# Windowed attention, forward and backward: y and z turned by a DMA transpose, the two products of dx stacked to K=128, eight PSUM banks in one ring

## The chip, the cores and the metric

The kernel runs on one core of one Trainium2 chip. The metric is the device time of one execution in microseconds (us), as a median over several executions. PSUM is the memory that PE writes its products to; the program hands it out as eight banks, and PE waits when no bank is free (before the change `pw` waited so 127 times, 40.0 us in all, for ACT to empty one). Engines: PE is TensorE, PEld its weight load, DVE is VectorE, ACT is ScalarE, POOL is GpSimd, SP is SyncE. SP computes nothing here; it issues DMA transfers. "SPq" in a profile line means that SP's sequencer is occupied.

## The reference, cut to what matters

The image is 256 x 256 tokens of 384 channels in bf16, cut into 1024 windows of 64 tokens.

```
qkv = xw @ wqkv                                    # xw: [1024 windows, 64, 384]
q, k, v = thirds of qkv
p = softmax(q k^T * 384**-0.5)
out = (p @ v) @ wo
# outputs: out, and the gradients for x, wqkv and wo, given grad_out
```

## The kernel before

Weights are merged at the start: A = wq wk^T * scale and B = wv wo. Write x for a window's tokens, g for its grad_out, P for the softmax and dS for the gradient of the scores. Then

- y is x A turned, z is g B^T turned, and u = x B, v = x A^T. y and z come out of PE as channels by tokens.
- scores are y^T x (for P) and z^T x (for dP).
- out = P u (PSUM tile `po`), and dx = P^T z + dS^T y + dS v, three products in one PSUM tile (`pd`). U = dS x (`pu`) and W = P^T g (`pw`) feed the weight gradients, which a "filler" stage accumulates (`pg`).

A tile is two windows (128 tokens) and a quad is four tiles. There are 128 quads, and each takes one step of a software pipeline. Scores need y and z as channels by tokens; `pd` needs them as tokens by channels. Before the change PE turned them, 24 transposes of 128x128 a quad, and DVE copied each group of three out of PSUM:

```python
def yz_tok(st, t, part):
    src, dst = ((st["yz"][:, :, t, 1:3, :], st["yq"]), (st["zc"][:, :, t, :, :], st["zq"]))[part]
    pt = ring.tile([P, CK, P], BF16, tag="r")
    for m in range(CK):
        nc.tensor.transpose(pt[:, m, :], src[:, m, :, :].rearrange("p w k -> p (w k)"), ident[:])
    nc.vector.tensor_copy(out=dst[:, t, :].rearrange("p (m c) -> p m c", m=CK), in_=pt[:])
```

Attention works on halves of 64 partitions. Four matmuls of the 64x64 array shape run side by side (their starts are within 0.01 us in the timeline below), two "straight" and two "crossed"; I call that a slot. A tile has three slots:

```python
both((po, "PT", "uq", True, True), (pd, "Pb", "zq", True, False))
... # po -> osb on ACT -> out_0, one DMA on SP
both((pu, "ST", "xq", True, True), (pd, "Sb", "yq", False, False))
... # pu -> Uq on DVE
both((pw, "Pb", "dq", True, True), (pd, "ST", "vq", False, True))
... # pd -> dsb on ACT -> out_1, two DMAs on POOL; pw -> Wq on DVE
```

The loads of a quad are four of x (SP) and four of grad_out (POOL), 96 KB each. Two DMA transposes on SP turn them into `xT` and `dT`.

Of the kernel before, what the change touches and what calls it, by code (L numbers as in the profile page):

```python
# [9 lines left out]
ALU = mybir.AluOpType  # L10
# [12 lines left out]
def kernel(  # L23
# [33 lines left out]
    qp = ctx.enter_context(tc.tile_pool(name="qp", bufs=2))  # L57
    sm = ctx.enter_context(tc.tile_pool(name="sm", bufs=2))
    ob = ctx.enter_context(tc.tile_pool(name="ob", bufs=3))
    ps_sd = ctx.enter_context(tc.tile_pool(name="ps_sd", bufs=1, space=bass.MemoryType.PSUM))  # L60
    ring = ctx.enter_context(tc.tile_pool(name="ring", bufs=7, space=bass.MemoryType.PSUM))

    ident = const.tile([P, P], BF16)
    make_identity(nc, ident[:])
# [43 lines left out]
        return ap[0, 2 * WIN * bp:2 * WIN * (bp + 1), WIN * t:WIN * (t + 1), :]  # L108

    LO, HI = slice(0, WT), slice(WT, P)  # L110

    def load(st):
        bp, t0 = st["at"]
        st["xq"] = xq = grp.tile([P, QUAD, C], BF16, tag="xq", name="xq", bufs=2 * GQ + 3)
        st["dq"] = dq = qp.tile([P, QUAD, C], BF16, tag="dq", name="dq", bufs=5)
        for t in range(QUAD):
            nc.sync.dma_start(out=xq[:, t, :], in_=dram_tile(x, bp, t0 + t))
            nc.gpsimd.dma_start(out=dq[:, t, :], in_=dram_tile(grad_out, bp, t0 + t))  # L118
        st["xT"] = xT = qp.tile([P, QUAD, CK, P], BF16, tag="xT", name="xT", bufs=3)
        st["dT"] = dT = qp.tile([P, QUAD, CK, P], BF16, tag="dT", name="dT")  # L120
        for src, dst in ((dq, dT), (xq, xT)):
            nc.sync.dma_start_transpose(out=dst[:].rearrange("p t m k -> p (t m) k"),
                                        in_=src[:].rearrange("p t c -> p (t c)"))

    ENG = {"D": nc.vector.tensor_copy, "A": nc.scalar.copy}

    def project(st, kind, mo):
        if kind == 0 and mo == 0:
            st["yz"] = qp.tile([P, CK, QUAD, 4, WT], BF16, tag="yz", name="yz")
            st["zc"] = qp.tile([P, CK, QUAD, 2, WT], BF16, tag="zc", name="zc")  # L130
        yz = st["yz"]
        wgt, src = ((BT_sb, st["dT"]), (A_sb, st["xT"]))[kind]
        pj = ring.tile([P, QUAD, 2, WT], F32, tag="r")
        for m in range(CK):
            nc.tensor.matmul(pj[:].rearrange("p t w k -> p (t w k)"), lhsT=wgt[:, m, mo * P:(mo + 1) * P],  # L135
                             rhs=src[:, :, m, :], start=(m == 0), stop=(m == CK - 1))
        if kind == 0:
            ENG[EV["z"][mo]](out=yz[:, mo, :, 0:4:3, :], in_=pj[:])  # L138
            nc.vector.tensor_copy(out=st["zc"][:, mo, :, :, :], in_=yz[:, mo, :, 0:4:3, :])
        else:  # L140
            ENG[EV["y"][mo]](out=yz[:, mo, :, 1:3, :], in_=pj[:])  # L141

    def scores(st):
        yz, xT = st["yz"], st["xT"]
        st["sd"] = sd = ps_sd.tile([P, QUAD, 2, WT], F32, tag="sd", name="sd")
        for t in range(QUAD):
            for w in range(2):
                for m in range(CK):
                    nc.tensor.matmul(sd[:, t, w, :],  # L149
                                     lhsT=yz[:, m, t, 2 * w:2 * w + 2, :].rearrange("p s k -> p (s k)"),  # L150
                                     rhs=xT[:, t, m, w * WT:(w + 1) * WT],
                                     start=(m == 0), stop=(m == CK - 1))
# [4 lines left out]
    def soft(st, step):  # L157
# [14 lines left out]
        elif step == 3:  # L172
# [4 lines left out]
            nc.vector.reciprocal(out=ri[:], in_=rs[:])  # L177
            st["Pb"] = Pb = qp.tile([P, QUAD, WT], BF16, tag="Pb", name="Pb")
            nc.vector.tensor_tensor(out=Pb[:], in0=ex[:], in1=over_k(ri[:]), op=ALU.mult)
        elif step == 4:  # L180
            st["pr"] = pr = sm.tile([P, QUAD, WT], F32, tag="pr", name="pr")
            for w, h in ((0, LO), (1, HI)):
                nc.vector.tensor_tensor(out=pr[h, :, :], in0=sd[h, :, w, :], in1=st["Pb"][h, :, :], op=ALU.mult)
            st["D"] = D = sm.tile([P, QUAD], F32, tag="D", name="D")
            nc.vector.tensor_reduce(out=D[:], in_=pr[:], axis=AX.X, op=ALU.add)
        else:
            pd = sm.tile([P, QUAD, WT], F32, tag="pd")
            nc.vector.tensor_tensor(out=pd[:], in0=st["Pb"][:], in1=over_k(st["D"][:]), op=ALU.mult)
            st["Sb"] = Sb = qp.tile([P, QUAD, WT], BF16, tag="Sb", name="Sb")
            nc.vector.tensor_tensor(out=Sb[:], in0=st["pr"][:], in1=pd[:], op=ALU.subtract)  # L190

    def uv(st, t, part):
        if t == 0 and part == 0:
            for n in ("uq", "vq", "yq", "zq"):
                st[n] = qp.tile([P, QUAD, C], BF16, tag=n, name=n)
        wgt, dst, cp = ((B_sb, st["uq"], ENG[EV["u"][t]]), (AT_sb, st["vq"], ENG[EV["v"][t]]))[part]
        pj = ring.tile([P, C], F32, tag="r")
# [2 lines left out]
                             start=(m == 0), stop=(m == CK - 1))  # L200
        cp(out=dst[:, t, :], in_=pj[:])  # L201

    def yz_tok(st, t, part):
        src, dst = ((st["yz"][:, :, t, 1:3, :], st["yq"]), (st["zc"][:, :, t, :, :], st["zq"]))[part]
        pt = ring.tile([P, CK, P], BF16, tag="r")
        for m in range(CK):
            nc.tensor.transpose(pt[:, m, :], src[:, m, :, :].rearrange("p w k -> p (w k)"), ident[:])  # L207
        nc.vector.tensor_copy(out=dst[:, t, :].rearrange("p (m c) -> p m c", m=CK), in_=pt[:])

    def turn(st, kind):  # L210
        src, n = ((st["Pb"], "PT"), (st["Sb"], "ST"))[kind]
        st[n] = dst = qp.tile([P, QUAD, WT], BF16, tag=n, name=n)
        pt = ring.tile([P, QUAD, WT], BF16, tag="r")
        for t in range(QUAD):
            for h in (LO, HI):
                nc.tensor.transpose(pt[h, t, :], src[h, t, :], ident[h, h])  # L216
        nc.vector.tensor_copy(out=dst[:], in_=pt[:])

    def attend(st, t):
        bp, t0 = st["at"]  # L220
        if t == 0:
            st["Uq"] = grp.tile([P, QUAD, C], BF16, tag="Uq", name="Uq")
            st["Wq"] = grp.tile([P, QUAD, C], BF16, tag="Wq", name="Wq")
        po = ring.tile([P, C], F32, tag="r", name="po")
        pd = ring.tile([P, C], F32, tag="r", name="pd")
        pu = ring.tile([P, C], F32, tag="r", name="pu")
        pw = ring.tile([P, C], F32, tag="r", name="pw")

        def both(straight, crossed):
            for h, o, (dst, lhs, rhs, first, last) in ((LO, LO, straight), (LO, HI, crossed), (HI, LO, crossed),  # L230
                                                       (HI, HI, straight)):
                nc.tensor.matmul(dst[o, :], lhsT=st[lhs][h, t, :], rhs=st[rhs][h, t, :], start=first, stop=last)  # L232

        both((po, "PT", "uq", True, True), (pd, "Pb", "zq", True, False))
        osb = ob.tile([P, C], BF16, tag="o")
        ENG[EV["o"][t]](out=osb[:], in_=po[:])  # L236
        nc.sync.dma_start(out=dram_tile(out_0, bp, t0 + t), in_=osb[:])
        both((pu, "ST", "xq", True, True), (pd, "Sb", "yq", False, False))
        ENG[EV["U"][t]](out=st["Uq"][:, t, :], in_=pu[:])  # L239
        both((pw, "Pb", "dq", True, True), (pd, "ST", "vq", False, True))  # L240
        dsb = ob.tile([P, C], BF16, tag="d")
        ENG[EV["d"][t]](out=dsb[:], in_=pd[:])  # L242
        for h, w in ((LO, 1), (HI, 0)):
            nc.gpsimd.dma_start(out=dram_tile(out_1, bp, t0 + t)[WIN * w:WIN * (w + 1)], in_=dsb[h, :])  # L244
        ENG[EV["W"][t]](out=st["Wq"][:, t, :], in_=pw[:])  # L245

    fill = []

# [19 lines left out]

    def step(c, b, a):

        def on(st):
            return (lambda f, *r: f(st, *r)) if st is not None else (lambda f, *r: None)
        C_, B, A = on(c), on(b), on(a)
# [5 lines left out]
        B(uv, 1, 0)  # L279
        B(uv, 1, 1)  # L280
        B(soft, 2)
        C_(attend, 0)
        B(soft, 3)
        C_(attend, 1)
        B(soft, 4)
        filler(1)
        B(uv, 2, 0)
        B(uv, 2, 1)
        B(soft, 5)
        B(uv, 3, 0)  # L290
        B(uv, 3, 1)
        for t in range(QUAD):
            B(yz_tok, t, 0)
            B(yz_tok, t, 1)
        C_(attend, 2)
        C_(attend, 3)
        B(turn, 0)
        B(turn, 1)
        for kind in range(2):
            for mo in range(CK):  # L300
                A(project, kind, mo)
        filler(1)

    EV = {"z": "AAA", "y": "DAD", "u": "AAAA", "v": "AAAA", "o": "AAAA", "U": "DDDD", "W": "DDDD", "d": "AAAA"}
    quads = [(bp, t0) for bp in range(NBP) for t0 in range(0, NT, QUAD)]
    sts = [{"at": q, "i": i} for i, q in enumerate(quads)]
    n = len(sts)
    AHEAD = 2
    with tc.manual_schedule(engines=MANUAL):
        for i in range(min(AHEAD, n)):  # L310
            load(sts[i])
        held = []
        get = lambda i: sts[i] if 0 <= i < n else None
        for i in range(-1, n + 1):
            if AHEAD <= i + AHEAD < n:
                load(sts[i + AHEAD])
            step(get(i - 1), get(i), get(i + 1))
            if i > 0:
                held.append(sts[i - 1])
# [65 lines left out]
```

## Time and profile before

| | before |
|---|---|
| median of 3 runs | 2295.58 us |
| period from scores to scores | 17.59 us, times 128 = 2251 us |
| PE stages of a period | u/v 3.99, filler 3.91, z and y 3.89, attention 3.13, y/z transposes 1.43, scores 0.70, P and dS transposes 0.53 |

The stage lengths are distances between the starts of stages in the PE timeline, averaged over the steady part. So each includes the wait, if any, before the next stage.

From the page: busy time of each engine, and the chain that ended last (the waits, followed back from the last instruction).

```profile
PE 2231.7 (97%) x22910; PEld 1334.9 (58%) x22910; DVE 1827.0 (80%) x4771; ACT 1259.5 (55%) x2701; POOL 867.2 (38%) x1542
...
PE 95%; ACT 3%; DVE 1%; issue 0%; DMA 0%; ACTq 0%
```

PE is the limit. The next view is PE's timeline in attention of tiles 0 and 1 (start, length, then the instructions).

```profile
1019.64 0.32 PE L232 MATMUL po<-uq,PT 64*64 64x384 bf16 x1
1019.64 0.33 PE L232 MATMUL pd<-zq,Pb 64*64 64x384 bf16 x2
1019.65 0.32 PE L232 MATMUL po<-uq,PT 64*64 64x384 bf16 x1
1019.80 0.32 PE L232 MATMUL pu<-xq,ST 64*64 64x384 bf16 x1
...
1020.45 0.32 PE L232 MATMUL pw<-dq,Pb 64*64 64x384 bf16 x1 [0.32 <-ACT osb L236]
```

From slot to slot it is 0.16 us (1019.64 to 1019.80), and the last slot comes 0.65 us after the one before it, because `pw` wants a PSUM bank that an ACT copy still has to empty. Instructions are listed as 0.32 us long, though the slots start 0.16 us apart, so the listed lengths overlap. Only the distances between starts count.

### The profile page before, as it was taken

What the parts mean: (1) busy time and instruction counts of PE and PEld (TensorE: products, weight loads), DVE (VectorE), ACT (ScalarE), POOL (GpSimd) and SP (SyncE); (2) the same over time, 40 slices, a digit from 0 to 9 for tenths busy, and PEclk for the clock granted to TensorE, in tenths of its full rate; (3) what the DMA queues carried; (4) which work ended last, traced back from release to release, by engine and by line L of the source; (5) the groups of instructions that cost most, each with busy time, mean ns of one, the idle gap of its engine ahead of it and who ended that gap; (6) DMA issues with size and microseconds to landing.
All of it is one profiled execution on the core that took longest, in us unless ns stands there. A gap on an engine that the chain in (4) does not pass through costs nothing.

```text
span 2293.8 us, 59316 instructions
## 1 busy us (share of the span) xinstructions
PE 2231.7 (97%) x22910; PEld 1334.9 (58%) x22910; DVE 1827.0 (80%) x4771; ACT 1259.5 (55%) x2701; POOL 867.2 (38%) x1542
## 2 busy tenths in 40 slices
PE   7999999999999999999999999999999999999998
PEld 4555555555555555555555555555555555555555
DVE  6878887888788878877887788778878887888786
ACT  4555555555555555555555555555555555555553
POOL 3443333334333343343334333433333343334332
PEclk9999999999999999999999999999999999999999
DMA  7666555665565556555656565656556655655542
GB/s 165 143 142 135 137 131 135 138 139 133 138 139 132 133 138 138 133 135 135 142 131 142 134 141 128 143 134 138 129 135 139 139 132 139 138 133 134 137 114 60
DMA packets 624475, 308.59 MB, mean 135 GB/s; under 512 B 458816, under 2 KB 607040, under 8 KB 624192
## 3 DMA queue, kind: packets, MB, share of 16 engines
q1 hardware_dynamic: 550064, 203.49, 42.1%
q0 software_dynamic: 73728, 101.02, 15.6%
q8 instruction: 179, 2.93, 0.5%
q14 instruction: 104, 0.85, 0.1%
q10 hardware_dynamic: 400, 0.29, 0.0%
HBM read 101.84 MB, written 101.84 MB: 89 GB/s over the span
## 4 chain that ended last, share of the span: by engine, by line
PE 95%; ACT 3%; DVE 1%; issue 0%; DMA 0%; ACTq 0%
PE pg L256 22%; PE pj L135 22%; PE pj L199 21%; PE pt L207 7%; PE po L232 5%; PE pw L232 5%; PE sd L149 4%; PE pd L232 3%; PE pu L232 2%; PE pt L216 2%; ACT osb L236 2%; PE pc L97 0%; ACT uq L201 0%; DMA w_sb<-in_wqkv_dram 0%; ACT vq L201 0%
## 5 line engine op out<-in xcount | busy, mean ns | idle before, releaser
L244 POOL DMA_DIRECT2D out_dram<-dsb x1024 | 575.9, 570 | 1388.2 <-ACT dsb L242 1365.6
L201 ACT CAST uq<-pj 128x384 bf16<-128x384 f32 x512 | 245.3, 479 | 635.1 <-PE pj L199 632.9
L256 PEld LDWEIGHTS <-xq 128*128 128x128 bf16 x3072 | 290.1, 98 | 217.3 <-issue 21.9
L199 PEld LDWEIGHTS <-xT 128*128 128x128 bf16 x3072 | 291.6, 98 | 182.3 <-issue 0.5
L239 DVE CAST Uq<-pu 128x384 bf16<-128x384 f32 x512 | 280.9, 549 | 80.2 <-PE pu L232 80.2
L236 ACT CAST osb<-po 128x384 bf16<-128x384 f32 x512 | 247.2, 483 | 163.0 <-PE po L232 146.2
L199 PE MATMUL pj<-B_sb,xT 128*128 128x384 bf16 x1536 | 333.5, 326 | 0.0
L199 PE MATMUL pj<-AT_sb,xT 128*128 128x384 bf16 x1536 | 333.3, 326 | 0.0
L118 POOL DMA_DIRECT2D dq<-in_grad_out_dram x512 | 291.8, 579 | 12.8 <-issue 11.4
L245 DVE CAST Wq<-pw 128x384 bf16<-128x384 f32 x512 | 279.4, 546 | 0.0
L138 ACT CAST yz<-pj 128x512 bf16<-128x512 f32 x384 | 225.1, 586 | 97.3 <-PE pj L135 81.6
L258 DVE TENSOR_TENSOR GF_acc<-pg,GF_acc 128x384 f32<-128x384 f32 x258 | 143.8, 557 | 167.7 <-PE pg L256 163.8
L256 PE MATMUL pg<-Uq,xq 128*128 128x384 bf16 x1536 | 271.2, 327 | 0.0
L135 PE MATMUL pj<-dT,BT_sb 128*128 128x512 bf16 x1152 | 270.8, 380 | 0.2
L256 PE MATMUL pg<-Wq,xq 128*128 128x384 bf16 x1536 | 270.5, 326 | 0.0
L135 PE MATMUL pj<-xT,A_sb 128*128 128x512 bf16 x1152 | 269.5, 379 | 0.0
L242 ACT CAST dsb<-pd 128x384 bf16<-128x384 f32 x512 | 251.9, 492 | 6.6 <-PE pw L232 0.3
L201 ACT CAST vq<-pj 128x384 bf16<-128x384 f32 x512 | 245.3, 479 | 4.3
L141 DVE CAST yz<-pj 128x512 bf16<-128x512 f32 x256 | 175.9, 687 | 55.4 <-PE pj L135 55.4
L232 PE MATMUL pw<-dq,Pb 64*64 64x384 bf16 x1024 | 179.7, 330 | 40.0 <-ACT osb L236 40.0
L232 PEld LDWEIGHTS <-ST 64*64 64x64 bf16 x2048 | 147.6, 104 | 113.0 <-issue 102.0
L232 PE MATMUL po<-uq,PT 64*64 64x384 bf16 x1024 | 203.5, 337 | 0.2
(72 smaller groups left out, 3487.6 us busy)
## 6 DMA issues: line engine op xcount, KB each, us to landing
xq<-in_x_dram SPq DMA_DIRECT2D x512, 96.0 KB, 3.1
dq<-in_grad_out_dram POOLq DMA_DIRECT2D x512, 96.0 KB, 2.8
out_dram<-osb SPq DMA_DIRECT2D x512, 96.0 KB, 2.7
out_dram<-dsb POOLq DMA_DIRECT2D x1024, 48.0 KB, 2.6
dT<-dq SPq DMA_TRANSPOSE x128, 4.0
xT<-xq SPq DMA_TRANSPOSE x128, 4.3
w_sb<-in_wqkv_dram SPq DMA_DIRECT2D x1, 864.0 KB, 5.7
out_dram<-dw_sb SPq DMA_DIRECT2D x1, 864.0 KB, 3.8
```

The source lines that it names most:

```text
L118: nc.gpsimd.dma_start(out=dq[:, t, :], in_=dram_tile(grad_out, bp, t0 + t))
L135: nc.tensor.matmul(pj[:].rearrange("p t w k -> p (t w k)"), lhsT=wgt[:, m, mo * P:(mo + 1) * P], rhs=src[:, :, m, :], start=(m == 0), stop ...
L138: ENG[EV["z"][mo]](out=yz[:, mo, :, 0:4:3, :], in_=pj[:])
L199: nc.tensor.matmul(pj[:], lhsT=st["xT"][:, t, m, :], rhs=wgt[:, m, :], start=(m == 0), stop=(m == CK - 1))
L201: cp(out=dst[:, t, :], in_=pj[:])
L232: nc.tensor.matmul(dst[o, :], lhsT=st[lhs][h, t, :], rhs=st[rhs][h, t, :], start=first, stop=last)
L236: ENG[EV["o"][t]](out=osb[:], in_=po[:])
L239: ENG[EV["U"][t]](out=st["Uq"][:, t, :], in_=pu[:])
L242: ENG[EV["d"][t]](out=dsb[:], in_=pd[:])
L244: nc.gpsimd.dma_start(out=dram_tile(out_1, bp, t0 + t)[WIN * w:WIN * (w + 1)], in_=dsb[h, :])
L245: ENG[EV["W"][t]](out=st["Wq"][:, t, :], in_=pw[:])
L256: nc.tensor.matmul(pw[:], lhsT=st["xq"][:, t, ma * P:(ma + 1) * P], rhs=st["UW"[f] + "q"][:, t, :], start=(i == 0), stop=(i == n - 1))
```

## The change

Intent: free PE of the 24 transposes and DVE of the copies. The DMA transpose works on the whole `yz` tile, whose token slots lie in the order z0 y0 y1 z1. Each turned block therefore holds z of a window in one half of the partitions and y in the other. P and dS are laid out the same way (`ps`), so that P^T z + dS^T y becomes one matmul with K=128. The changed core, with cuts marked:

```diff
-    ps_sd = ... bufs=1, PSUM          # a bank of its own for the scores
-    ring = ... bufs=7, PSUM
+    ring = ... bufs=8, PSUM
     # load
-            nc.gpsimd.dma_start(out=dq[:, t, :], in_=dram_tile(grad_out, bp, t0 + t))
+            nc.sync.dma_start(out=dq[:, t, :], in_=dram_tile(grad_out, bp, t0 + t))
     # project: no zc copies any more
+    def to_tokens(st):
+        st["tok"] = tok = qp.tile([P, CK, QUAD, 2, P], BF16, tag="tok", name="tok")
+        nc.sync.dma_start_transpose(out=tok[:].rearrange("p m t b k -> p (m t b) k"),
+                                    in_=st["yz"][:].rearrange("p m t s k -> p (m t s k)"))
     # soft, step 3
+            for w, h in ((0, LO), (1, HI)):
+                nc.scalar.copy(out=ps[h, w, :, :], in_=Pb[h, :, :])
     # soft, step 5
-            nc.vector.tensor_tensor(out=Sb[:], in0=st["pr"][:], in1=pd[:], op=ALU.subtract)
+            for w, h, o in ((0, LO, HI), (1, HI, LO)):
+                nc.vector.tensor_tensor(out=ps[o, w, :, :], in0=st["pr"][h, :, :], in1=pd[h, :, :], op=ALU.subtract)
     # attend, now for a pair of tiles
+        for t in pair:
+            pd = ring.tile([P, C], F32, tag="r", name="pd")
+            for w, o in ((0, HI), (1, LO)):
+                nc.tensor.matmul(pd[o, :], lhsT=st["ps"][:, w, t, :], rhs=st["tok"][:, :, t, w, :], start=True,
+                                 stop=False)
+        ... # then for each tile: (pu, po), (pw, pd += dS v) as two slots of 64x64
+                    nc.gpsimd.dma_start(...)     # out_0 and out_1, four stores of 48 KB a tile, all on POOL
     # step: u/v, z, filler, attention of tiles 2 and 3, P/dS transposes, y, transpose to tokens, filler,
     #       attention of tiles 0 and 1
-    EV = {..., "y": "DAD", ...}
+    EV = {..., "y": "AAA", ...}
-    AHEAD = 2
+    AHEAD = 3
```

The four loads of grad_out moved from POOL's queue to SP's, and the stores of out_0 from SP's to POOL's. Cut above: there is one more buffer for grad_out (6) and for x, and the transposes of x and grad_out are issued one step after their loads.

More of the change, by code (lines that the diff above doesn't have):

```diff
@@ L59 @@
     ob = ctx.enter_context(tc.tile_pool(name="ob", bufs=3))
-    ps_sd = ctx.enter_context(tc.tile_pool(name="ps_sd", bufs=1, space=bass.MemoryType.PSUM))
-    ring = ctx.enter_context(tc.tile_pool(name="ring", bufs=7, space=bass.MemoryType.PSUM))
+    ring = ctx.enter_context(tc.tile_pool(name="ring", bufs=8, space=bass.MemoryType.PSUM))
     ident = const.tile([P, P], BF16)
@@ L110, with load_turn @@
     LO, HI = slice(0, WT), slice(WT, P)
+    OTHER = {0: HI, WT: LO}
     def load(st):
         bp, t0 = st["at"]
-        st["xq"] = xq = grp.tile([P, QUAD, C], BF16, tag="xq", name="xq", bufs=2 * GQ + 3)
-        st["dq"] = dq = qp.tile([P, QUAD, C], BF16, tag="dq", name="dq", bufs=5)
+        st["xq"] = xq = grp.tile([P, QUAD, C], BF16, tag="xq", name="xq", bufs=2 * GQ + 4)
+        st["dq"] = dq = qp.tile([P, QUAD, C], BF16, tag="dq", name="dq", bufs=6)
         for t in range(QUAD):
             nc.sync.dma_start(out=xq[:, t, :], in_=dram_tile(x, bp, t0 + t))
-            nc.gpsimd.dma_start(out=dq[:, t, :], in_=dram_tile(grad_out, bp, t0 + t))
+            nc.sync.dma_start(out=dq[:, t, :], in_=dram_tile(grad_out, bp, t0 + t))
+    def load_turn(st):
+        xq, dq = st["xq"], st["dq"]
         st["xT"] = xT = qp.tile([P, QUAD, CK, P], BF16, tag="xT", name="xT", bufs=3)
@@ L121, in load, with grad_turn @@
         for src, dst in ((dq, dT), (xq, xT)):
-            nc.sync.dma_start_transpose(out=dst[:].rearrange("p t m k -> p (t m) k"),
-                                        in_=src[:].rearrange("p t c -> p (t c)"))
+            k = G_ON_PE if src is dq else 0
+            if k < QUAD:
+                nc.sync.dma_start_transpose(out=dst[:, k:].rearrange("p t m k -> p (t m) k"),
+                                            in_=src[:, k:].rearrange("p t c -> p (t c)"))
+    def grad_turn(st, t):
+        if t >= G_ON_PE:
+            return
+        pt = ring.tile([P, CK, P], BF16, tag="r")
+        for m in range(CK):
+            nc.tensor.transpose(pt[:, m, :], st["dq"][:, t, m * P:(m + 1) * P], ident[:])
+        nc.vector.tensor_copy(out=st["dT"][:, t, :, :], in_=pt[:])
     ENG = {"D": nc.vector.tensor_copy, "A": nc.scalar.copy}
@@ L129, in project @@
             st["yz"] = qp.tile([P, CK, QUAD, 4, WT], BF16, tag="yz", name="yz")
-            st["zc"] = qp.tile([P, CK, QUAD, 2, WT], BF16, tag="zc", name="zc")
         yz = st["yz"]
@@ L138, in project @@
             ENG[EV["z"][mo]](out=yz[:, mo, :, 0:4:3, :], in_=pj[:])
-            nc.vector.tensor_copy(out=st["zc"][:, mo, :, :, :], in_=yz[:, mo, :, 0:4:3, :])
         else:
             ENG[EV["y"][mo]](out=yz[:, mo, :, 1:3, :], in_=pj[:])
+    def to_tokens(st):
+        st["tok"] = tok = qp.tile([P, CK, QUAD, 2, P], BF16, tag="tok", name="tok")
+        nc.sync.dma_start_transpose(out=tok[:].rearrange("p m t b k -> p (m t b) k"),
+                                    in_=st["yz"][:].rearrange("p m t s k -> p (m t s k)"))
     def scores(st):
         yz, xT = st["yz"], st["xT"]
-        st["sd"] = sd = ps_sd.tile([P, QUAD, 2, WT], F32, tag="sd", name="sd")
+        st["sd"] = sd = ring.tile([P, QUAD, 2, WT], F32, tag="r", name="sd")
         for t in range(QUAD):
@@ L179, in soft @@
             nc.vector.tensor_tensor(out=Pb[:], in0=ex[:], in1=over_k(ri[:]), op=ALU.mult)
+            st["ps"] = ps = qp.tile([P, 2, QUAD, WT], BF16, tag="ps", name="ps")
+            for w, h in ((0, LO), (1, HI)):
+                nc.scalar.copy(out=ps[h, w, :, :], in_=Pb[h, :, :])
         elif step == 4:
@@ L188, in soft @@
             nc.vector.tensor_tensor(out=pd[:], in0=st["Pb"][:], in1=over_k(st["D"][:]), op=ALU.mult)
-            st["Sb"] = Sb = qp.tile([P, QUAD, WT], BF16, tag="Sb", name="Sb")
-            nc.vector.tensor_tensor(out=Sb[:], in0=st["pr"][:], in1=pd[:], op=ALU.subtract)
+            ps = st["ps"]
+            for w, h, o in ((0, LO, HI), (1, HI, LO)):
+                nc.vector.tensor_tensor(out=ps[o, w, :, :], in0=st["pr"][h, :, :], in1=pd[h, :, :], op=ALU.subtract)
     def uv(st, t, part):
         if t == 0 and part == 0:
-            for n in ("uq", "vq", "yq", "zq"):
+            for n in ("uq", "vq"):
                 st[n] = qp.tile([P, QUAD, C], BF16, tag=n, name=n)
@@ L201, in uv @@
         cp(out=dst[:, t, :], in_=pj[:])
-    def yz_tok(st, t, part):
-        src, dst = ((st["yz"][:, :, t, 1:3, :], st["yq"]), (st["zc"][:, :, t, :, :], st["zq"]))[part]
-        pt = ring.tile([P, CK, P], BF16, tag="r")
-        for m in range(CK):
-            nc.tensor.transpose(pt[:, m, :], src[:, m, :, :].rearrange("p w k -> p (w k)"), ident[:])
-        nc.vector.tensor_copy(out=dst[:, t, :].rearrange("p (m c) -> p m c", m=CK), in_=pt[:])
     def turn(st, kind):
-        src, n = ((st["Pb"], "PT"), (st["Sb"], "ST"))[kind]
+        n = ("PT", "ST")[kind]
         st[n] = dst = qp.tile([P, QUAD, WT], BF16, tag=n, name=n)
@@ L214, in turn, with attend @@
         for t in range(QUAD):
-            for h in (LO, HI):
-                nc.tensor.transpose(pt[h, t, :], src[h, t, :], ident[h, h])
+            for w, o, h in ((0, LO, HI), (1, HI, LO)):
+                if kind == 0:
+                    nc.tensor.transpose(pt[o, t, :], st["Pb"][o, t, :], ident[o, o])
+                else:
+                    nc.tensor.transpose(pt[o, t, :], st["ps"][h, w, t, :], ident[h, h])
         nc.vector.tensor_copy(out=dst[:], in_=pt[:])
-    def attend(st, t):
+    def attend(st, pair):
@@ L220, in attend @@
         bp, t0 = st["at"]
-        if t == 0:
+        if pair[0] == 0:
             st["Uq"] = grp.tile([P, QUAD, C], BF16, tag="Uq", name="Uq")
             st["Wq"] = grp.tile([P, QUAD, C], BF16, tag="Wq", name="Wq")
-        po = ring.tile([P, C], F32, tag="r", name="po")
-        pd = ring.tile([P, C], F32, tag="r", name="pd")
-        pu = ring.tile([P, C], F32, tag="r", name="pu")
-        pw = ring.tile([P, C], F32, tag="r", name="pw")
-        def both(straight, crossed):
-            for h, o, (dst, lhs, rhs, first, last) in ((LO, LO, straight), (LO, HI, crossed), (HI, LO, crossed),
-                                                       (HI, HI, straight)):
-                nc.tensor.matmul(dst[o, :], lhsT=st[lhs][h, t, :], rhs=st[rhs][h, t, :], start=first, stop=last)
@@ L234, in attend @@
-        both((po, "PT", "uq", True, True), (pd, "Pb", "zq", True, False))
-        osb = ob.tile([P, C], BF16, tag="o")
-        ENG[EV["o"][t]](out=osb[:], in_=po[:])
-        nc.sync.dma_start(out=dram_tile(out_0, bp, t0 + t), in_=osb[:])
-        both((pu, "ST", "xq", True, True), (pd, "Sb", "yq", False, False))
-        ENG[EV["U"][t]](out=st["Uq"][:, t, :], in_=pu[:])
-        both((pw, "Pb", "dq", True, True), (pd, "ST", "vq", False, True))
-        dsb = ob.tile([P, C], BF16, tag="d")
-        ENG[EV["d"][t]](out=dsb[:], in_=pd[:])
@@ L243, in attend @@
-        for h, w in ((LO, 1), (HI, 0)):
-            nc.gpsimd.dma_start(out=dram_tile(out_1, bp, t0 + t)[WIN * w:WIN * (w + 1)], in_=dsb[h, :])
-        ENG[EV["W"][t]](out=st["Wq"][:, t, :], in_=pw[:])
+        pds = []
+        for t in pair:
[3 more added lines that the diff above has]
+                                 stop=False)
+            pds.append(pd)
@@ new lines, in both @@
+        def both(t, straight, crossed):
+            for h, o, (dst, lhs, rhs, first) in ((LO, LO, straight), (LO, HI, crossed), (HI, LO, crossed),
+                                                 (HI, HI, straight)):
+                nc.tensor.matmul(dst[o, :], lhsT=st[lhs][h, t, :], rhs=st[rhs][h, t, :], start=first, stop=True)
+        for t, pd in zip(pair, pds):
+            po = ring.tile([P, C], F32, tag="r", name="po")
+            pu = ring.tile([P, C], F32, tag="r", name="pu")
+            pw = ring.tile([P, C], F32, tag="r", name="pw")
+            both(t, (pu, "ST", "xq", True), (po, "PT", "uq", True))
+            osb = ob.tile([P, C], BF16, tag="o")
+            ENG[EV["o"][t]](out=osb[:], in_=po[:])
+            ENG[EV["U"][t]](out=st["Uq"][:, t, :], in_=pu[:])
+            both(t, (pw, "Pb", "dq", True), (pd, "ST", "vq", False))
+            dsb = ob.tile([P, C], BF16, tag="d")
+            ENG[EV["d"][t]](out=dsb[:], in_=pd[:])
+            for dst, src in ((out_0, osb), (out_1, dsb)):
+                for h, w in ((LO, 1), (HI, 0)):
+                    nc.gpsimd.dma_start(out=dram_tile(dst, bp, t0 + t)[WIN * w:WIN * (w + 1)], in_=src[h, :])
+            ENG[EV["W"][t]](out=st["Wq"][:, t, :], in_=pw[:])
@@ L281, in step @@
         B(soft, 2)
-        C_(attend, 0)
         B(soft, 3)
-        C_(attend, 1)
-        B(soft, 4)
-        filler(1)
         B(uv, 2, 0)
         B(uv, 2, 1)
-        B(soft, 5)
+        for t in range(QUAD):
+            A(grad_turn, t)
         B(uv, 3, 0)
         B(uv, 3, 1)
-        for t in range(QUAD):
-            B(yz_tok, t, 0)
-            B(yz_tok, t, 1)
-        C_(attend, 2)
-        C_(attend, 3)
+        B(soft, 4)
+        for mo in range(CK):
+            A(project, 0, mo)
+        B(soft, 5)
+        filler(1)
+        C_(attend, (2, 3))
         B(turn, 0)
         B(turn, 1)
-        for kind in range(2):
-            for mo in range(CK):
-                A(project, kind, mo)
+        for mo in range(CK):
+            A(project, 1, mo)
+        A(to_tokens)
         filler(1)
-    EV = {"z": "AAA", "y": "DAD", "u": "AAAA", "v": "AAAA", "o": "AAAA", "U": "DDDD", "W": "DDDD", "d": "AAAA"}
+        B(attend, (0, 1))
+    G_ON_PE = 0
+    EV = {"z": "AAA", "y": "AAA", "u": "AAAA", "v": "AAAA", "o": "AAAA", "U": "DDDD", "W": "DDDD", "d": "AAAA"}
     quads = [(bp, t0) for bp in range(NBP) for t0 in range(0, NT, QUAD)]
@@ L311 @@
             load(sts[i])
+            if i < AHEAD - 1:
+                load_turn(sts[i])
         held = []
@@ L316 @@
                 load(sts[i + AHEAD])
+            if AHEAD - 1 <= i + AHEAD - 1 < n:
+                load_turn(sts[i + AHEAD - 1])
             step(get(i - 1), get(i), get(i + 1))
```

## The prediction

> **What bounds the kernel now.** TensorE. The page gives PE 97% busy, DVE 80%, ACT 55%, and the chain of waits is 95% PE. In the timeline the period from one scores stage to the next is 17.59 us (1016.38 to 1033.97); 128 quads make 2251 us, and about 42 us are prologue and tail. Per quad, by distances between starts in the PE timeline: scores 0.70 us, u/v 8 x 0.488 = 3.90, the gradient filler 2 x 1.95 = 3.90, projections 3.89, the y/z transposes 1.34 (24 x 56 ns), the P/dS transposes 0.53, and attention 12 slots of four 64x64 matmuls. A slot takes 0.16 us when nothing holds it (1.92 in all), but attention fills about 3.3 us: tiles 0 and 1 lose 0.48 us waiting for a PSUM bank (the pw matmul waits for the osb copy 127 times), and tiles 2 and 3 go at 0.26 us instead of 0.16, the pace of the DVE's eight yq/zq copies before them (started every 0.265 us), which free the banks.
>
> **What goes.** The y/z transposes, 1.34 us of PE; eight yq/zq copies (345 ns each) and three zc copies (294 ns); two 687 ns yz casts move to ACT. DVE falls from 14.2 to about 10 us a quad. The bank pacing, about 1.0 us of PE, should mostly go with it, helped by eight banks in one ring.
>
> **What stays.** Stacking saves no streaming time: the two pd products sat in slots that po and pu shared. Before, a tile needs three slots of four 64x64 matmuls; after, one of two 128x64 and two of four 64x64.
>
> **What comes.** (1) Two more changes of array shape per quad[...]. In this trace, entering or leaving attention shows 0.09 to 0.13 us extra, so I add 0.2 us. (2) ACT takes two 64x256 copies (estimate 0.4 us each) and two casts of 0.59 us: 9.9 to about 12 us. (3) One transpose of 768 KB per quad. The two existing ones (384 KB each) run at about 205 GB/s, 256-byte packets of 18 ns median, so some 3.9 us more DMA engine time: from roughly 9 to 13 us of a 16 us period. It is issued some 14 us before attention reads it, so its latency should not show. (4) out_0 moves to POOL: 16 issues of 0.57 us, 9.1 us. None becomes the longest engine.
>
> **Sum for PE.** Streaming 14.85 us, shape changes 0.5, left-over bank waits 0.3: 15.7 us. Times 128 plus 44: **2055 us**, 10% faster. Range 1985 to 2150. Chances: faster by over 2% 0.92, within 2% 0.05, slower 0.03.
>
> **What would show it right or wrong.** PE near 97% busy with a period near 15.7 us; no yq/zq/zc groups; DVE near 65%, ACT near 75%; attention slots at 0.16 us with the osb wait gone; the stacked pair of matmuls starting together; nobody waiting for the tok transpose; DMA share near 0.8.
>
> **What would make it wrong.** The two 128x64 matmuls of a tile not running side by side, or their weight loads not hidden: up to 0.16 us per tile, 80 us in all. DMA: if transposes, loads and stores slow each other, tok or xT/dT arrive late and PE waits, perhaps above 2150 us. ACT: the P copies sit in its queue before four u/v evictions and wait for DVE's softmax, which could run the banks out and stall PE.

The 0.2 us is my estimate from the 0.09 to 0.13 us that stand there (before the change, 1018.55 to 1019.13 us into attention, where three matmuls of u/v take 0.49 us; 1020.45 to 1020.74 out of it, where a slot takes 0.16). Point (2) does not say what its 0.4 us rests on. ACT's one operation of 256 elements took 0.42 us before the change (419 ns, L171), and the copies took 0.40 us in the changed kernel (403 ns, L198).

## More of the kernel before

The SP queue, from the view of one tile's instructions: shortest, median and longest issue in ns, then the start of the first and the last in us.

```profile
L122 SPq DMA_TRANSPOSE dT<-dq x128: 1435/1471/2642, 9.1 to 2213.8; - x128
L122 SPq DMA_TRANSPOSE xT<-xq x128: 1412/1665/3262, 11.0 to 2215.4; - x128
L117 SPq DMA_DIRECT2D xq<-in_x_dram x512: 552/598/2314, 1.3 to 2209.8; - x171
```

So each load holds SP for 0.60 us and a transpose of 12 blocks of 128x128 for 1.47 us (`dT`) or 1.67 us (`xT`), by the medians. Over a quad SP was issuing for 8.6 us out of 17.6 (the lengths of all its DMA instructions, added up).

## The result, and the profile after

The changed kernel takes 2143.5 us (median of 4 runs, 2137.1 to 2146.7) against 2295.9 us. The ratio is 0.9333, with a 95% interval of 0.9308 to 0.9358. Ratios here are the mean time of one kernel's fast runs over that of the other's of the same rounds, so not quite the ratio of the medians. The time lies inside the stated range, 88 us above the number that I gave.

Stage lengths a quad, computed from the traces as before, in us:

| | u/v | z | y | filler | attention | P/dS transp. | y/z transp. | scores | period |
|---|---|---|---|---|---|---|---|---|---|
| before | 3.99 | 1.95 | 1.94 | 3.91 | 3.13 | 0.53 | 1.43 | 0.70 | 17.59 |
| after | 4.42 | 1.97 | 1.94 | 4.09 | 2.84 | 0.38 | 0 | 0.70 | 16.33 |

Without any wait u/v takes 3.90 us, the least in this trace. So the changed kernel has a floor of about 15.8 us on PE, and 0.54 us is lost between u/v and z. The page after, in the same order as before:

```profile
PE 2029.8 (95%) x18814; PEld 1098.6 (51%) x18814; DVE 1379.5 (64%) x3235; ACT 1448.5 (68%) x3213; POOL 1137.8 (53%) x2054
...
DMA  8999999999999999999999999999999999999992
...
PE 41%; DMA 26%; SPq 15%; ACT 9%; issue 5%; POOL 1%; DVE 1%; ACTq 0%; POOLq 0%
DMA dT<-dq 20%; PE pj L147 16%; PE pj L219 10%; PE pg L278 9%; SPq L117 7%; SPq L118 7%; DMA out_dram<-osb 5%; ACT yz L150 4%; ACT osb L259 3%; PE sd L165 3%; POOL out_dram L266 1%; SPq L156 1%; DMA out_dram<-dsb 1%; ACT yz L152 1%; PE pd L244 1%
```

The chain that ended last is no longer PE's alone: it passes through the landing of `dT` and through SP's issue of loads (L117, L118). PE's timeline shows the place, the end of u/v and the start of z:

```profile
1023.46 0.65 PE L219 MATMUL pj<-AT_sb,xT 128*128 128x384 bf16 x3
1024.90 2.12 PE L147 MATMUL pj<-dT,BT_sb 128*128 128x512 bf16 x9 [0.79 <-DMA dT<-dq]
```

SP's timeline over one quad explains it:

```profile
1006.75 6.27 SPq L156 DMA_TRANSPOSE tok<-yz  x1
1013.06 0.59 SPq L117 DMA_DIRECT2D xq<-in_x_dram  x1
1013.69 0.60 SPq L118 DMA_DIRECT2D dq<-in_grad_out_dram  x1
1014.33 0.60 SPq L117 DMA_DIRECT2D xq<-in_x_dram  x1
1014.97 0.60 SPq L118 DMA_DIRECT2D dq<-in_grad_out_dram  x1
1015.61 0.60 SPq L117 DMA_DIRECT2D xq<-in_x_dram  x1
1016.26 0.60 SPq L118 DMA_DIRECT2D dq<-in_grad_out_dram  x1
1016.90 0.60 SPq L117 DMA_DIRECT2D xq<-in_x_dram  x1
1017.54 0.62 SPq L118 DMA_DIRECT2D dq<-in_grad_out_dram  x1
1018.20 2.17 SPq L127 DMA_TRANSPOSE dT<-dq  x1
1020.42 1.99 SPq L127 DMA_TRANSPOSE xT<-xq  x1
1022.51 5.35 SPq L156 DMA_TRANSPOSE tok<-yz  x1
```

There is no hole in it. Each issue starts 0.04 to 0.10 us after the one before it ends. From `tok` to `tok` it is 15.76 us here, and on average SP is inside a DMA instruction for 15.7 us of a period of 16.3; the gaps between eleven instructions make up the rest. The transposes that fill it take longer than they did before:

```profile
L127 SPq DMA_TRANSPOSE dT<-dq x128: 1439/2204/3315, 9.7 to 2076.3; - x128
L127 SPq DMA_TRANSPOSE xT<-xq x128: 1715/2778/4687, 11.4 to 2077.8; - x128
L156 SPq DMA_TRANSPOSE tok<-yz x128: 3603/5592/7426, 30.2 to 2099.0; - x128
```

Two more numbers that I computed from the trace say who waits for whom. The transpose to tokens starts on average 6.4 us after the last copy of y that it needs has ended, so SP is late and not y. And in 85 of 128 quads z starts within 0.1 us of the landing of `dT`.

A trap for readers of waits: the view of SP's waits puts 578 us of `tok` down to an ACT copy.

```profile
SPq L156 <- ACT yz L150: 578.1, 115, 6.3
```

That is a copy of z (L150) in the stage that runs meanwhile. The copies of y, on which the transpose depends, had long been done. The 5.0 us that it lists for each of the 115 is about as long as the issue of the transpose itself (5.5 us on average).

### The profile page after: what moved, and what is told of

It is laid out like the page before. It is cut to its first block, busy times and chain, and to the rows that moved or that the text cites. A ratio compares the mean times of both kernels' runs of the same rounds, so it can differ in the third digit from the quotient of the medians.

```text
span 2144.9 us, 50954 instructions
## 1 busy us (share of the span) xinstructions
PE 2029.8 (95%) x18814; PEld 1098.6 (51%) x18814; DVE 1379.5 (64%) x3235; ACT 1448.5 (68%) x3213; POOL 1137.8 (53%) x2054
## 3 DMA queue, kind: packets, MB, share of 16 engines
q8 instruction: 147, 2.41, 0.5%
## 4 chain that ended last, share of the span: by engine, by line
PE 41%; DMA 26%; SPq 15%; ACT 9%; issue 5%; POOL 1%; DVE 1%; ACTq 0%; POOLq 0%
DMA dT<-dq 20%; PE pj L147 16%; PE pj L219 10%; PE pg L278 9%; SPq L117 7%; SPq L118 7%; DMA out_dram<-osb 5%; ACT yz L150 4%; ACT osb L259 3%; PE sd L165 3%; POOL out_dram L266 1%; SPq L156 1%; DMA out_dram<-dsb 1%; ACT yz L152 1%; PE pd L244 1%
## 5 line engine op out<-in xcount | busy, mean ns | idle before, releaser
L266 POOL DMA_DIRECT2D out_dram<-osb x1024 | 571.9, 563 | 933.6 <-ACT osb L259 906.3
L278 PEld LDWEIGHTS <-xq 128*128 128x128 bf16 x3072 | 300.0, 98 | 226.8 <-issue 1.6
L147 PE MATMUL pj<-dT,BT_sb 128*128 128x512 bf16 x1152 | 276.6, 387 | 60.4 <-DMA dT<-dq 54.2
L221 ACT CAST vq<-pj 128x384 bf16<-128x384 f32 x512 | 250.2, 489 | 2.8 <-PE pj L219 0.5
L152 ACT CAST yz<-pj 128x512 bf16<-128x512 f32 x384 | 224.2, 585 | 32.0 <-PE pj L147 0.9
L150 ACT CAST yz<-pj 128x512 bf16<-128x512 f32 x384 | 208.4, 638 | 14.4 <-PE pj L147 13.3
L147 PEld LDWEIGHTS <-BT_sb 128*128 128x128 bf16 x1152 | 106.8, 99 | 207.2 <-DMA dT<-dq 92.2
L198 ACT COPY ps<-Pb 64x256 bf16<-64x256 bf16 x256 | 103.2, 403 | 149.6 <-DVE Pb L195 148.1
L251 PE MATMUL pu<-xq,ST 64*64 64x384 bf16 x1024 | 175.5, 336 | 0.0
```

The lines of the kernel that those rows point to most:

```text
L147: nc.tensor.matmul(pj[:].rearrange("p t w k -> p (t w k)"), lhsT=wgt[:, m, mo * P:(mo + 1) * P], rhs=src[:, :, m, :], start=(m == 0), stop ...
L150: ENG[EV["z"][mo]](out=yz[:, mo, :, 0:4:3, :], in_=pj[:])
L152: ENG[EV["y"][mo]](out=yz[:, mo, :, 1:3, :], in_=pj[:])
L221: cp(out=dst[:, t, :], in_=pj[:])
L251: nc.tensor.matmul(dst[o, :], lhsT=st[lhs][h, t, :], rhs=st[rhs][h, t, :], start=first, stop=True)
L266: nc.gpsimd.dma_start(out=dram_tile(dst, bp, t0 + t)[WIN * w:WIN * (w + 1)], in_=src[h, :])
```

## The experiments

Theories, stated before the first runs. Q: SP's queue, which issues one transfer after the other, has become a second bottleneck. D: the 16 DMA engines are full (the page's DMA row shows 9 everywhere). B: the lost time is a wait for PSUM banks or for ACT, since the trace also names ACT before z in places. All edits are to the changed kernel unless another is named.

### 1. The loads of grad_out back on POOL

```diff
-            nc.sync.dma_start(out=dq[:, t, :], in_=dram_tile(grad_out, bp, t0 + t))
+            nc.gpsimd.dma_start(out=dq[:, t, :], in_=dram_tile(grad_out, bp, t0 + t))
```

> The changed kernel with one line undone: the four dq loads of a quad are issued on POOL again, as before the change, so SP issues 4 loads and 3 transposes instead of 8 and 3. Theory Q (the SP queue, which issues one transfer after the other, is the co-bottleneck: 8 loads of 0.64 us and three transposes of together about 11 us make a loop of 16.1 us, longer than PE's own 15.8): the loop falls to 13.5 us, the dT wait of 0.54 us per quad goes, the period is PE's 15.8 us and the time 2075 us. Theory D (the 16 DMA engines themselves are full): same bytes and packets, so 2143 us within 1% and the dT wait stays. Theory B (the wait is for PSUM banks or ACT, as the chain also names ACT ps before the z projection): no change either.

Measured: 2082.5 us (2080.7 to 2085.8), ratio 0.9075, correct. SP is issuing for 12.2 us of a period of 15.9. Its timeline now has holes, 1003.10 to 1015.89 being the whole of its work for one quad:

```profile
1003.10 4.96 SPq L156 DMA_TRANSPOSE tok<-yz  x1
1008.10 2.53 SPq L117 DMA_DIRECT2D xq<-in_x_dram  x4
1010.80 2.13 SPq L127 DMA_TRANSPOSE dT<-dq  x1
1012.98 2.91 SPq L127 DMA_TRANSPOSE xT<-xq  x1
```

The transpose to tokens starts 0.03 us after the last y copy in every quad of the steady part, and `dT` lands in the median 9.1 us before z reads it, in no quad within 0.1 us. One line, with the same bytes moved, returns 61 of the 88 us. D, which expected no change, is refuted in the form that was stated, and the DMA row shows how little it tells. The windows view of 200 to 2000 us, for the changed kernel first and then for this run (last columns: granted clock, DMA share, GB/s):

```profile
200.00:2000.00 1800.00, 1725.93 (x16115) 933.52 (x16113) 1173.34 (x2754) 1238.80 (x2754) 978.08 (x1763) 1.00 1.02 195
```

```profile
200.00:2000.00 1800.00, 1761.07 (x16501) 962.61 (x16500) 1202.76 (x2825) 1263.16 (x2825) 1251.79 (x2260) 1.00 1.08 200
```

The share was above 1 in both (1.02 and 1.08), so the packet times that it adds up overlap, and it was higher in the faster run. Two things besides SP's time changed with that line: the loads went to POOL's own DMA queue, and there in fewer packets (the traces show 1536 and 4608 bytes where SP's loads have 768), so the expectation's "same bytes and packets" is half true. The engines' time did not fall with it, as the share shows. Run 4 keeps queue and packet size.

### 2. No transpose to tokens (wrong result)

```diff
-        st["tok"] = tok = qp.tile(...); nc.sync.dma_start_transpose(out=tok..., in_=yz...)
+        st["tok"] = tok_fixed            # set to zero once
```

> Wrong result on purpose: the changed kernel without the tok transpose; attention reads a tile of zeros that is set once. Everything else as it is. It takes the new DMA work away whole. Theories Q and D both expect the dT wait to go and about 2075 us (PE's own 15.8 us a quad). If the time stays near 2143 us (theory B), the missing half microsecond per quad has nothing to do with DMA.

Measured: 2070.2 us (2068.9 to 2071.6), ratio 0.902. As meant, out_1 (dx) is wrong and the other outputs are right. u/v to z is 3.92 us, and the period is 15.82. This is what PE can do in this arrangement; my number for it was 2055.

### 3. The same layout by PE transposes

```diff
-        nc.sync.dma_start_transpose(out=tok..., in_=yz...)
+        for t in range(QUAD):
+            for b in range(2):
+                pt = ring.tile([P, CK, P], BF16, tag="r")
+                for m in range(CK):
+                    nc.tensor.transpose(pt[:, m, :], yz[:, m, t, 2 * b:2 * b + 2, :]..., ident[:])
+                nc.vector.tensor_copy(out=tok[:, :, t, b, :], in_=pt[:])
     # called in one row after the z stage
```

> The changed kernel with the tok layout made by 24 PE transposes and 8 DVE copies per quad, as y and z were before, but in the stacked layout. It leaves the stacking, the order of the stages and the ring of eight banks, and takes the DMA transpose away. Expected by Q and D: PE 15.8 + 1.34 us of transposes, no dT wait, some bank waits behind the 8 copies of 0.35 us: period 17.1 to 17.5 us, 2250 to 2290 us, correct result. Then the new order and ring alone bring at most 2%, and the DMA transpose the rest. If it is below 2200 us, the order and ring bring more than I think.

Measured: 2331.8 us (2330.5 to 2335.4), ratio 1.0162, correct. That is above my range. The 24 transposes took 2.08 us where 24 x 56 ns make 1.34. Run 7 repairs this.

### 4. Four more issues on SP, no more bytes

```diff
-            nc.sync.dma_start(out=dq[:, t, :], in_=dram_tile(grad_out, bp, t0 + t))
+            for r in range(2):
+                nc.sync.dma_start(out=dq[WT * r:WT * (r + 1), t, :],
+                                  in_=dram_tile(grad_out, bp, t0 + t)[WIN * r:WIN * (r + 1)])
```

> The suspected cost doubled in part: the changed kernel with each of the four dq loads cut into two issues of 64 partitions on SP. Same bytes, same packet size, four more issues per quad. Theory Q: the SP loop grows by 4 x 0.64 us to about 18.7 us and the time to about 2440 us. Theory D: the engines have the same packets to move, so within 1% of 2143 us. Theory B: no change.

Measured: 2347.6 us (2343.6 to 2362.1), ratio 1.0239: slower than before the change, with the bytes of the changed kernel. An issue of half a load (0.63 us) costs as much as one of a whole load (0.60 us):

```profile
1009.21 1.26 SPq L119 DMA_DIRECT2D dq<-in_grad_out_dram  x2
```

The period is 17.96 us, where Q expected 18.7, so 1.6 of the 2.6 us came through. The rest was won back in the transposes: `tok` held SP for 4.9 us on average instead of 5.5. So the transposes' part of SP's loop is not a fixed cost. It gets shorter when they come further apart, which fits that SP waits in them for the DMA engines. No run shows that wait by itself. Two readings of the traces bear on it. In run 4, the quarter of the `tok` issues with the least other traffic in its first 3.6 us took 4.1 us on average and the quarter with the most 5.6; in the changed kernel these are 5.3 and 5.6. And in the changed kernel's `tok` shown above, the engines moved only 9 GB/s from 1011.0 to 1012.0 us, so full engines cannot be all of it.

### 5. Four staging buffers in place of three, with grad_out on POOL

```diff
 # on top of experiment 1
-    ob = ctx.enter_context(tc.tile_pool(name="ob", bufs=3))
+    ob = ctx.enter_context(tc.tile_pool(name="ob", bufs=4))
```

> The changed kernel with the dq loads on POOL (as in the first of the experiments) and four instead of three staging buffers for each output tile. In that first experiment 13 waits of PE, together about 15 us, were left, of 0.3 to 2.8 us each, and ACT waited 63 us for output stores to free a staging buffer. If those are the cause, the time falls from 2083 to about 2070 us, what the run without the tok transpose took. If not, it stays at 2083.

Measured: 2066.0 us (2063.0 to 2071.4), ratio 0.9003, correct. The period is 15.79 us. u/v to z is 3.90 us in every quad of the steady part, so no wait is left there.

### 6. Stacking undone, DMA transpose kept

With the slots in the order z0 y0 y1 z1, taking the stacked matmul apart would give a straight and a crossed product into one `pd` bank. The two straight products of `po` read different halves of the input partitions and write the two partition halves of one bank; their starts are 0.01 us apart (1019.64 and 1019.65 above), and the result is correct. No run here shows what the chip does when two such products write the same half. So DVE sorts the slots first, and all `pd` products are crossed, as before the change:

```diff
 # on top of experiment 5
+    def sort(st, kind):                       # zy holds z0 z1 y0 y1
+        for mo in range(CK):
+            nc.vector.tensor_copy(out=st["zy"][:, mo, :, 2 * kind:2 * kind + 2, :],
+                                  in_=st["yz"][:, mo, :, (slice(0, 4, 3), slice(1, 3))[kind], :])
-    in_=st["yz"]...                           # to_tokens
+    in_=st["zy"]...
-    two ACT copies into ps; two DVE subtracts into ps
     # yz has one buffer in place of two, to make room for zy
+    one DVE subtract into Sb
-    attend: pd, pd stacked; then (pu, po), (pw, pd) for each tile
+    attend: (pu, pd += P z) for both tiles; (po, pd += dS y) for both; (pw, pd += dS v) for both
```

> The kernel of the run above with the stacking undone and the DMA transpose kept: z and y are copied by the DVE (6 copies of about 0.29 us) into the order z0 z1 y0 y1, one DMA transpose turns them, and all three pd products are 64x64 matmuls beside po, pu and pw, as before the change. No array-shape change inside attention; pu is made and released first, so that the next stage finds a bank. Stage lengths in the changed kernel: attention takes 1.42 us a pair, of which 6 slots are 0.96; 0.13 goes for the change from 128x64 to 64x64 and about 0.16 for the bank wait at its end. If stacking only costs (my view), attention falls to about 1.15 us a pair and the time from about 2070 to about 2000 us. If stacking helps PE (the intent of the change), it rises above 2070 us.

Measured: 2033.0 us (2019.3 to 2049.7), ratio 0.8837, correct. The execution of 2049.7 us counts as slow, being 1.5% above the fastest; the ratio leaves it out, and the three others have a median of 2024.5 us. Attention falls from 2.84 to 2.41 us a quad, and the P/dS transposes rise from 0.38 to 0.48. The timeline of one pair after the change and the start of the next stage (instructions of one slot cut to the first):

```profile
1000.99 0.52 PE L244 MATMUL pd<-tok,ps 128*64 128x384 bf16 x4
1001.44 0.35 PE L251 MATMUL pu<-xq,ST 64*64 64x384 bf16 x1
...
1001.63 0.32 PE L251 MATMUL pw<-dq,Pb 64*64 64x384 bf16 x1
...
1001.79 0.32 PE L251 MATMUL pu<-xq,ST 64*64 64x384 bf16 x1
...
1001.95 0.32 PE L251 MATMUL pw<-dq,Pb 64*64 64x384 bf16 x1
...
1002.41 0.86 PE L165 MATMUL sd<-xT,yz 128*128 128x64 bf16 x24
```

And the same pair unstacked:

```profile
1003.60 0.35 PE L245 MATMUL pu<-xq,ST 64*64 64x384 bf16 x1
...
1003.79 0.32 PE L245 MATMUL pu<-xq,ST 64*64 64x384 bf16 x1
1003.95 0.32 PE L245 MATMUL po<-uq,PT 64*64 64x384 bf16 x1
...
1004.11 0.33 PE L245 MATMUL pd<-tok,Sb 64*64 64x384 bf16 x2
...
1004.27 0.32 PE L245 MATMUL pw<-dq,Pb 64*64 64x384 bf16 x1
...
1004.44 0.32 PE L245 MATMUL pw<-dq,Pb 64*64 64x384 bf16 x1
1004.78 0.86 PE L172 MATMUL sd<-xT,yz 128*128 128x64 bf16 x24
```

Stacked, the two 128x64 slots take 0.45 us before the first 64x64 slot starts, where the first two slots of the unstacked pair take 0.35 (1003.60 to 1003.95). I put the 0.10 down to the shape change. From the last slot to scores it is 0.46 us stacked and 0.34 unstacked. Both have six slots, and the pair takes 1.42 against 1.18 us. The unstacked run also releases its first bank earlier, and ACT has two copies less to make, so it shows shape change, order of the products, bank wait and ACT's relief together; no run separates them.

### 7. PE transposes, spread out

```diff
 # experiment 3, with its eight groups called one at a time:
+    after u/v tiles 1 and 2 (four groups), after each z projection (three), after soft 5 (one)
```

> The run with the PE transposes again (2332 us, above what I expected), with the eight groups of transposes spread between the u/v and z stages instead of in one row behind z. There the row of 24 took 2.05 us instead of the 1.34 that 24 x 56 ns make, and that 0.7 us a quad is the excess. If it is only the wait for banks behind the evictions, the period falls from 17.9 to about 17.2 us and the time to 2240 to 2260 us. If it stays at 2330, the stacked order with PE transposes is slower for another reason.

Measured: 2237.2 us (2235.5 to 2237.6), ratio 0.9745, correct. The transposes take 1.36 us a quad and the period is 17.16. So the excess in run 3 was my placement, behind evictions that held the banks. With a fair placement, everything in the change except the DMA transpose brings 2.5%.

### 8. Four staging buffers alone

```diff
 # on the changed kernel
-    ... name="ob", bufs=3
+    ... name="ob", bufs=4
```

> The changed kernel with four staging buffers for each output tile and nothing else. ACT waits 181 us for output stores to free a staging buffer in the changed kernel. Theory Q (SP's issue loop sets the period): no change, 2143 us within 1%. Theory B (banks and ACT): towards 2075 us.

Measured: 2136.7 us (2135.1 to 2145.2), ratio 0.932 against 0.9333 of the changed kernel: no difference clear of noise, and z waits for `dT` as before. So B is refuted as far as the staging buffers go; run 1, which removes most of the wait and changes neither banks nor ACT's work, speaks against the rest of it. The staging buffers mattered only once SP was relieved (run 5 against run 1).

### 9 to 11. What makes the unstacked kernel uneven

```diff
 # 9: on top of 6                       # 10: on top of 6            # 11: on top of 6
-    ob bufs=4; dq bufs=6               -    dq bufs=6               -    nc.gpsimd.dma_start(out=dq...
+    ob bufs=6; dq bufs=5               +    dq bufs=5               +    (nc.gpsimd, nc.sync)[t % 2].dma_start(out=dq...
```

> The unstacked kernel with six instead of four staging buffers for each output tile (and five dq buffers instead of six, to make room). Its four runs spread from 2019 to 2050 us, its median period is 15.39 us but its mean 15.60, and ACT waited 72 us and 34 us for output stores to free staging buffers. If these waits are the rest, the mean period comes to 15.4 and the time to 2020 us, with a smaller spread. If POOL, which issues stores and dq loads in one row, is what makes it uneven, it stays at 2030 or gets worse by the missing dq buffer.

> The unstacked kernel (2033 us) with five dq buffers instead of six, and its four staging buffers. The run before this changed both counts at once and came to 2100 us. If the missing dq buffer did that (the loads are then issued late, in POOL's row behind the stores), this run is near 2100 us too; if the two more staging buffers did it, it stays near 2033 us.

> The unstacked kernel with two of the four dq loads of a quad on POOL and two on SP. SP's issue time rises from 12.7 to about 14.0 us a quad, POOL's falls from 11.2 to about 10.1, both below PE's 15.4. If POOL's row is what makes the unstacked kernel uneven (mean period 15.60 against a median of 15.39), the mean comes down to 15.4 and the time to about 2020 us; if SP at 14.0 of 15.4 already is too full, it rises above 2033 us.

Measured: run 9 2100.6 us (2089.4 to 2105.1), run 10 2032.3 us (2028.0 to 2038.7), run 11 2029.5 us (2025.7 to 2031.0, ratio 0.8835). All are correct. Run 9 went against what I expected, and run 10 clears the missing dq buffer (its 2032.3 us are within 0.4% of the 2024.5 of run 6's fast executions). So it was six staging buffers in place of four that cost 68 us. Why is open: the trace of run 9 shows ACT waiting 108 us for out_1 stores to free a staging buffer (34 us in run 6) and `tok` holding SP for 5.9 us instead of 5.0, but no run tells cause from effect. Run 11 has a mean period of 15.46 us, close to the median of 15.39, though SP is issuing for 14.9 us of it; its time is the same as run 6's within the intervals, so what makes run 6 uneven stays open. Run 11 beats both kernels: 11.6% below before and 5.3% below the changed kernel (1 minus 2029.5 / 2295.9, and 2029.5 / 2143.5).

## Why the prediction was right or wrong

The direction was right. The time lay in the range partly by luck: 6.5 us below its upper end, brought there by a bottleneck that the prediction does not have. Point by point:

- **"What bounds the kernel now. TensorE."** Right; the chain was 95% PE.
- **PE's sum, 15.7 us a quad.** Right: 15.79 in run 5, where nothing else holds PE. "Shape changes 0.5, left-over bank waits 0.3" comes close: attention is 2.84 us a quad against 1.92 us of slots, so 0.9 us over. The filler grew as well, from 3.91 to 4.09 us, and the P/dS transposes shrank from 0.53 to 0.38, neither of which was forecast; that the two nearly cancel is luck.
- **"Stacking saves no streaming time."** Right: six slots of about 0.16 us in both forms. That it costs is likely but not shown by itself: unstacked, with the order of the products and ACT's copies changed as well, run 6 is 1.8% faster (0.8837 / 0.9003). The 0.10 us at the change from 128x64 to 64x64 fits; its cause was not shown.
- **"The bank pacing ... should mostly go."** Right for the slots: the `pw` wait is gone and 64x64 slots stand 0.16 to 0.19 us apart. The 1.0 us did not come: attention fell by only 0.29 us, from 3.13 to 2.84, the rest being taken up by the 0.10 us a pair that I put down to the shape change and by 0.46 us in place of 0.16 at the end of each pair.
- **"(3) ... None becomes the longest engine." "nobody waiting for the tok transpose."** This is the step that failed. I costed the new transpose on the 16 DMA engines (3.9 us, at 205 GB/s; while `tok` ran alone the engines moved 287 GB/s, changed kernel, 1012.5 to 1014.5 us) and its latency (14 us to spare), and looked at POOL's issue time, but never at SP's. SP took on four loads of grad_out (2.5 us a quad) and a transpose of 24 blocks, and lost four stores of out_0 (2.7 us). So loads and stores together hold SP for as long as before (5.3 and 5.1 us a quad), and the growth from 8.6 to 15.7 us is all in the transposes, 3.3 to 10.6 us. At the lengths of before I would have got 8 x 0.60 + 1.47 + 1.67 + about 2.9 (twice a transpose of 12 blocks) = 10.8 us, which still fits under the 15.7 us that I had for PE. It is the stretch of the transposes, to 2.2, 2.8 and 5.5 us, that made the sum as long as PE's own period. Nobody waits long for `tok`, true; but `dT` is issued in the same queue behind it, and PE waits for `dT`, 0.54 us a quad.
- **The missing 88 us** (92 in the profiled execution, of 2146.7 us) are 0.54 x 128 = 69 us of that wait, 0.09 x 128 = 12 us of PE's sum (15.79 against 15.70), and about 11 us of start and end (2145 minus 128 x 16.33 is 55 us, I had 44). Run 1 returns 61 us by taking four issues off SP, and run 5 returns 77.
- **"DMA share near 0.8."** Wrong: 1.02 in the steady part. The number turned out to mean little, since it was 1.08 in the faster run 1. PE is 95% busy (97 was forecast), DVE 64% (65) and ACT 68% (75), and the two matmuls of a stacked pair start together, 3 ns apart.
- **"What would make it wrong ... DMA: ... xT/dT arrive late and PE waits."** The symptom was named, the path was not: runs 1 and 4 show that the issues on SP count. The transposes' stretch may be the slowing of transfers by each other that is named here; which share of it is, no run shows. The first risk did not come true (the pair starts together), nor the ACT risk (the P copies in its queue); in run 5 they are there and z never waits.

How the gain splits: all but the DMA transpose 2.5% (run 7), with the DMA transpose 6.7%, with SP relieved 10.0% (run 5), unstacked 11.6%. These are steps between whole kernels in this order; run 5 also has the fourth staging buffer.

## What to carry to other kernels

When work moves to DMA, make one more column in the budget: issue time per issuing engine, count of transfers times the length of one, transposes included. Leave room in it, since transposes got longer here under load: with the lengths of before the column reads 10.8 us, and 15.7 were measured. A queue without holes in its timeline is a suspect. In the changed kernel it was one to blame (15.7 of 16.3 us, and run 1 returned 61 us). But run 11 has a queue almost as full (14.9 of 15.5 us) and is no slower than run 6 with holes in it, so an experiment has to decide. To tell it from full DMA engines, split a transfer into two issues of half the size, or move some to another queue: the bytes stay and the issues change. Splitting is the cleaner of the two, since a move to POOL's queue changed the packet sizes as well (run 1: 1536 and 4608 bytes in place of 768).
